# LayerNorm of the last 1024 tokens from x handed over in feature rows, in a fused attention and MLP kernel

## The chip, the cores and the metric

One core of a Trainium2 chip runs the whole kernel in one launch. The metric is the device time of one execution in microseconds (us): the median of 3 runs of the kernel before is 1620.89 us (1620.71 to 1621.32). The core's engines are TensorE (PE; its weight loads are PEld), VectorE (DVE), ScalarE (ACT), GpSimd (POOL) and SyncE (SP), which issues the DMAs here.

## The reference

```python
# x: [1, 2048, 512], 32 heads of 16; all float32
xn = (x - mean(x, -1)) / sqrt(var(x, -1) + 1e-5)
qkv = (xn @ wqkv).reshape(B, S, 3, H, Dh)            # wqkv: [512, 1536]
p = softmax(q @ k.T * Dh ** -0.5)                     # per head
s = (p @ v) @ wo                                      # wo: [512, 512]
h = xn @ w1 + b1; h = where(h > 0, h, 0) ** 2         # w1: [512, 1792]
g = silu(h @ w2 + b2)                                 # w2: [1792, 512]
return x + s * g
```

The inputs are drawn at random, x and the weights with a spread of 0.05, and b2 is multiplied by 3.878.

## The kernel before

Every float32 product is made of three matmuls in a reduced type: each operand is split in a high part (a copy, rounded) and a low part (what is left), and high x high, high x low and low x high are added up in PSUM. A product over 512 features takes 4 feature blocks x 3 = 12 matmuls.

The kernel has three stages. In the first one LayerNorm and some of the QKV projection are done. The 2048 tokens are 16 tiles of 128 (t = 0 to 15) and 4 chunks of 512 (c = 0 to 3). For each tile `load_x` brings x with tokens in rows, `ln_stats` takes mean and variance on VectorE (BN_STATS, BN_AGGR) and a square root on ScalarE, `ln_norm` normalizes, `ln_high` turns the tile with four TensorE transposes into PSUM (`pm_t`) and copies the high part to `xTs[c]` with ScalarE, and `ln_low` makes the low part with VectorE. `xTs[c]` has features in rows, as the projection needs them.

Between these the function `pump(n)` emits n matmuls of the projections that already have their tokens: `qk_tile(4, c)` makes K and `qk_tile(0, c)` Q of the first eight heads for chunk c (m = 4 and 0, 12 matmuls of 512 columns; chunk 0 is done in halves of 256 columns), `v_tile` makes V of one tile. They write to three PSUM banks of the pool `pe` in turn (`se`), and a bank is free when its result has been copied out. K and Q are split (`hl`), stored to DRAM (`k_d`, `q_d`), and read back in rows of heads: `load_k` fills the K tiles `ka` (12 DMAs, one row group of 16 partitions each), `load_q` the Q tiles `qm`. V goes to `v_d`. The normalized x is also copied to DRAM for the MLP (`spill`, to `xn_d`).

The second stage, the lead, interleaves the rest of the projections (L1157) with the first attention scores (L320), whose row maxima VectorE takes (L327). The third and longest stage is attention, and the MLP and output products between it.

PE, ACT, DVE and POOL run in the order in which the code is written. In the first stage the order of the DMAs on SP's queue is chosen when the program is built; SP then issues them strictly in that order, and a DMA that has to wait for a semaphore holds up all behind it. In the program each DMA also waits until the one that used its semaphore before (eight semaphores in turn) has landed.

The loop of the first stage is this, cut:

```python
for i in range(NT + 3):
    ...
    if i < NT:
        ln_stats(i)
    if 0 <= i - 1 < NT:
        ln_norm(i - 1)
    if 2 <= i - 3 < NT:
        ln_low(i - 3)
    if 0 <= i - 2 < NT:
        ln_high(i - 2)
```

Of the kernel before, what the change touches and what calls it, by code (L numbers as in the profile page):

```python
# [9 lines left out]
F32 = mybir.dt.float32  # L10
F32R = mybir.dt.float32r
AF = mybir.ActivationFunctionType
# [5 lines left out]
P = 128  # L18
S = 2048
# [13 lines left out]
NPT = 17  # L33
NVT = 7
NXR = 16
EVAC = (1, 6, 7, 9, 11, 14)
GAPS = (24,)
FIRST = 2
W1_LOADS = (13, 14, 16, 20, 23)
SPILLS = (5, 9, 13, 17)  # L40
LAST_MAX = 486
RUN = 454
PAIR = (484, 485)
# [14 lines left out]
def kernel(  # L58
# [6 lines left out]
    b1: bass.AP,  # L65
    w2: bass.AP,
    b2: bass.AP,
    out: bass.AP,
):
    nc = tc.nc  # L70
# [8 lines left out]
    r_d = [dram.tile([4, 512], F32, name=f"r_d{u}") for u in range(NU)]  # L79
    on_d = [dram.tile([2, P, S], F32, name=f"on_d{k}") for k in range(KO)]  # L80
    sp_d = dram.tile([S, D], F32, name="sp_d")
    xn_d = dram.tile([2, P, KO, S], F32, name="xn_d")
    v_d = dram.tile([P, NT, H * VW], F32, name="v_d")
    g_d = dram.tile([S, D], F32, name="g_d")
# [30 lines left out]
    with ExitStack() as ph:  # L115
# [39 lines left out]
                    src_d[h // 8][i, (h % 8) * DH : (h % 8 + 1) * DH, cols],  # L155
                )

        def load_k(qd, n):

            p, j, i = n // 6, n // 3 % 2, n % 3  # L160
            if n % 6 == 0:
                kas[qd, p] = ring("ka")
            h = 4 * qd + 2 * p + j
            nc.sync.dma_start(
                kas[qd, p][64 * j + DH * i : 64 * j + DH * (i + 1), :].bitcast(F32),
                k_d[h // 8][i % 2, (h % 8) * DH : (h % 8 + 1) * DH, :],
            )

        def load_v(qd):
# [830 lines left out]
        def load_w(name, width, parts):  # L1000
            raw = st.tile([P, KO, width], F32, name=name)
            at = 0
            for c0, n in parts:
                nc.sync.dma_start(raw[:, :, at : at + n], w_in[:, :, c0 : c0 + n])
                at += n
            return raw
# [11 lines left out]
        def qk_terms(m, c, ps):  # L1018
            wq, m0 = wq_cols(m)
            ms = slice(m0, m0 + P)  # L1020
            xT = xTs[c]
            t = terms3(ps, [
                (lambda a, q, ko=ko: wq[q, a, ko, ms], lambda b, q, ko=ko: xT[q, b, ko])
                for ko in range(KO)
            ])
            if m == 4 and c == 0:

                t = [t[k] for k in (0, 3, 6, 9, 2, 5, 1, 4, 7, 10, 8, 11)]
            return t

# [180 lines left out]
        xts = {}  # L1211

        def load_x(t):
            xts[t] = xp.tile([P, D], F32, name="xt", bufs=12)
            nc.sync.dma_start(xts[t], xf[t * P : (t + 1) * P, :])

        mvs = {}
        rstds = {}
        pts_ = {}

        def ln_stats(t):
            stats = xp.tile([P, 6], F32, name="stats")
            nc.vector.bn_stats(stats, xts[t])
            mvs[t] = xp.tile([P, 2], F32, name="mv", bufs=3)
            nc.vector.bn_aggr(mvs[t], stats)
            rstds[t] = xp.tile([P, 2], F32, name="rstd", bufs=3)
            nc.scalar.activation(rstds[t][:, 0:1], mvs[t][:, 1:2], AF.Sqrt, bias=eps_t)

        def ln_norm(t):
# [12 lines left out]
            xts[t] = xn  # L1242

        def ln_high(t):
            xn, xT = xts.pop(t), xTs[t // 4]
            pt = pm.tile([P, 512], F32, name="pm_t").rearrange("p (k n) -> p k n", n=P)
            for ko in range(KO):
                nc.tensor.transpose(pt[:, ko, :], xn[:, ko * P : (ko + 1) * P], ident)  # L1248
            sl = slice((t % 4) * P, (t % 4 + 1) * P)
            nc.scalar.activation(xT[:, 0, :, sl], pt, AF.Copy)  # L1250
            pts_[t] = pt
# [63 lines left out]
        make_ring("ka", kp, range(2), S)  # L1315
        for t in range(2):
            load_x(t)
        raw_m = load_w("wm", 2 * P, ((0, P), (D, P)))
        for t in range(2, 6):
            load_x(t)  # L1320
        raw_v = load_w("wv", D, ((2 * D, D),))
        for t in range(6, NT):
            load_x(t)
        for vt in vts:
            nc.vector.memset(vt[:, :, DH:], 1.0)
        fill_ring("ka", 0, -1.0)
        for i in range(NT + 3):
            if i in (2, 3):

                kos = slice(2 * i - 4, 2 * i - 2)  # L1330
                if i == 2:
                    ln_norm(1)
                    ln_high(0)
                    split_w(wa_t, kos, slice(0, 2 * P), raw_m[:, kos])
                    ln_low(0)
                else:
                    ln_high(1)
                    split_w(wa_t, kos, slice(0, 2 * P), raw_m[:, kos])
                    ln_stats(2)
                    ln_low(1)  # L1340
                    ln_norm(2)
                    ln_stats(3)
            else:
                if i < NT:
                    ln_stats(i)
                if 0 <= i - 1 < NT:
                    ln_norm(i - 1)
                if 2 <= i - 3 < NT:
                    ln_low(i - 3)
                if i == 4:  # L1350

                    pump(10)
                if 0 <= i - 2 < NT:
# [6 lines left out]
            if i in (11, 12):  # L1360
                fill_ring("qm", i - 11, 0.0)
            if i == 11:
                raw_r = [load_w("wv", 3 * P, ((P, 3 * P),))]
            if i in (13, 14):
                spill(0, i - 13)
            if i in (16, 18):
                spill(1, (i - 16) // 2)
            if i >= 4:
                pump({4: 6, 7: 14, 8: 12}.get(i, 8 if i < 7 else 7 if i < 11 else 6))
            if i == 3:  # L1370
                ahead.append(qk_first())
            if i >= 7 and (i - 3) % 4 == 3:
                c = (i - 3) // 4
                ahead.append(qk_tile(4, c))
                rest.append(qk_tile(0, c))
                order.append(("qk", 0, c))
            if i >= 3 and (i - 3) % 4 == 3:
                c = (i - 3) // 4
                rest += [v_tile(c, tt) for tt in range(4)]
                order += [("v", c, tt) for tt in range(4)]  # L1380
        let_go()
        hold[0] = False
        while ahead:
# [2 lines left out]
        kp2 = ph.enter_context(tc.tile_pool(name="kp2", bufs=1))  # L1386
        make_ring("ka", kp2, (2, 3), S)
        make_ring("qe", kp2, range(4), 512)
        for k in range(2):
# [5 lines left out]
            b1_t, b1.rearrange("(fo p) -> p fo", p=P), allow_slow_non_contiguous=True  # L1395
        )
        nc.sync.dma_start(b2_t, b2[None, :].to_broadcast([P, D]))
        for ko in range(KO):
            split_w(wr_t, ko, slice(0, 3 * P), raw_r[0][:, ko])
        for n in range(12):  # L1400
            load_k(0, n)
        qms[0] = load_q(0, "qm")
        fill_ring("qm", 2, 0.0)
        for n in range(4):
            fill_ring("qe", n, 0.0)
        fill_ring("ka", 2, -1.0)
        pump(47)
        led.append(0)
        at = order.index(("v", 2, 0)) + 1
        while len(rest) > len(order) - at:  # L1410
# [24 lines left out]
        def lead_rounds():  # L1435
            for i in side_rounds(specs, single):
                if i % 6 == 0:
                    now[0] = i // 6
                    run_waiting()
                    if i // 6 in SPILLS:  # L1440
                        c, k = divmod(SPILLS.index(i // 6), 2)
                        spill(c + 2, k)
# [263 lines left out]
        wstk.close()  # L1706


_INS = ['A_x', 'A_wqkv', 'A_wo', 'B_w1', 'B_b1', 'B_w2', 'B_b2']
_OUTS = [((1, 2048, 512), 'float32')]  # L1710


# [20 lines left out]
```

## Time and profile before

| | before |
|---|---|
| median of 3 runs | 1620.89 us (1620.71 to 1621.32) |
| profiled execution | 1621.38 us, span 1619.6 us, granted clock 1.00 |
| PE busy | 1607.3 us (99%) |
| PEld | 939.7 us (58%) |
| DVE | 1352.4 us (84%) |
| ACT | 1187.2 us (73%) |
| POOL | 534.1 us (33%) |
| chain that ended last | PE 99%, DVE 1% |
| first lead matmul (L1157) | 62.94 us after the span's start |

The profile is one execution; its times are counted from the start of the span, and 1.8 us of its 1621.38 us lie outside the span. A busy PE is not PE at its peak, since matmuls are pipelined. The chain that ended last is followed back from the last instruction, at each step to what released it. The queue of SP counts as no engine; the row of a DMA issue has the time that SP spent on it, waits for room in the queue included.

### The profile page before, as it was taken

Reading aid. Unit: us, or ns where it says so; the run is one execution under the profiler, and the core shown is the slowest. Engines: PE = TensorE matmul, PEld = TensorE weight load, DVE = VectorE, ACT = ScalarE, POOL = GpSimd, SP = SyncE. Lnnn points to the kernel's source line nnn. Section 1 sums busy time; section 2 is a strip of 40 time slices with the busy share of each in tenths; the row PEclk is TensorE's granted clock in tenths of the full one; section 3 lists DMA queues with packets and bytes.
Section 4 is the critical chain, followed back from the end, with each engine's and each line's share of the span. In section 5 each row is a group of like instructions: output and inputs, shape, how many; then the busy total and the mean of one; then the engine's idle time right before and its main releaser. Section 6 shows DMA issues by size and latency. Waiting matters only on the chain.

```text
span 1619.6 us, 36065 instructions
## 1 busy us (share of the span) xinstructions
PE 1607.3 (99%) x13660; PEld 939.7 (58%) x13660; DVE 1352.4 (84%) x2307; ACT 1187.2 (73%) x2347; POOL 534.1 (33%) x610
## 2 busy tenths in 40 slices
PE   8999999999999999999999999999999999999998
PEld 7799665556545654664466446645654565445543
DVE  7486888888888888888888888888888888887754
ACT  7212777777777777877777777777777777778886
POOL 6436667133113311331133113311331123214621
PEclk9999999999999999999999999999999999999999
DMA  8967556434333333423333334323432252237655
GB/s 290 244 237 234 174 156 160 132 96 128 81 104 94 106 88 88 131 87 101 90 107 100 91 89 118 115 71 90 131 107 73 65 163 76 64 102 228 207 177 169
DMA packets 164173, 209.19 MB, mean 129 GB/s; under 512 B 59136, under 2 KB 79360, under 8 KB 162432
## 3 DMA queue, kind: packets, MB, share of 16 engines
q1 hardware_dynamic: 163856, 206.63, 43.9%
q8 instruction: 108, 1.77, 0.5%
q14 instruction: 65, 0.53, 0.1%
q10 hardware_dynamic: 144, 0.26, 0.0%
HBM read 148.90 MB, written 56.34 MB: 127 GB/s over the span
## 4 chain that ended last, share of the span: by engine, by line
PE 99%; DVE 1%; DMA 0%; issue 0%; ACT 0%; DVEq 0%
PE po L406 31%; PE pd_t L258 19%; PE pm_t L320 17%; PE se L1286 15%; PE pd_t L226 5%; PE pm_t L1157 4%; PE pm_t L226 1%; PE pd_t L1157 1%; PE se L1127 1%; PE se L1061 1%; PE se L320 1%; PE pm_t L1248 0%; PE pd_t L1127 0%; DVE mx L327 0%; PE po L1061 0%; DMA xt<-in_A_x_dram 0%
## 5 line engine op out<-in xcount | busy, mean ns | idle before, releaser
L327 DVE TENSOR_REDUCE mx<-pm_t 128x1 f32<-128x512 f32 x1910 | 1188.3, 684 | 174.5 <-PE pm_t L320 84.8
L1298 ACT ACTIVATE pt<-se 128x512 f32<-128x512 f32 x1894 | 975.4, 613 | 234.3 <-PE se L1286 187.0
L320 PE MATMUL pm_t<-ka,qm 64*128 64x512 f32 x1910 | 761.0, 419 | 0.0
L1286 PE MATMUL se<-qe,ka 64*128 64x512 f32 x2005 | 677.3, 396 | 0.0
L406 PE MATMUL po<-pt,v 128*32 128x512 f32 x3820 | 520.8, 605 | 0.2 <-DVE tsm L849 0.2
L320 PEld LDWEIGHTS pm_t<-ka,qm 64*128 64x128 f32 x1910 | 335.2, 184 | 236.0 <-DVE mx L327 224.5
L1286 PEld LDWEIGHTS se<-qe,ka 64*128 64x128 f32 x2005 | 338.9, 184 | 19.8 <-ACT xr L1298 1.7
L258 PEld LDWEIGHTS pd_t<-xc,w1s 64*128 64x128 f32 x2352 | 292.1, 187 | 82.2 <-issue 82.2
L258 PE MATMUL pd_t<-xc,w1s 64*128 64x256 f32 x2352 | 332.3, 288 | 0.0
L258 PE MATMUL pd_t<-w2t,hT 64*128 64x512 f32 x1080 | 300.1, 410 | 0.0
L258 PEld LDWEIGHTS pd_t<-w2t,hT 64*128 64x128 f32 x1080 | 179.3, 184 | 82.4 <-issue 75.5
L571 POOL TENSOR_TENSOR r<-r 128x512 f32<-128x512 f32 x56 | 58.2, 1040 | 353.5 <-ACT r L568 353.5
L406 PEld LDWEIGHTS po<-pt,v 128*32 128x32 f32 x3820 | 76.7, 108 | 147.1 <-issue 125.6
L327 DVE TENSOR_REDUCE mx<-se 128x1 f32<-128x512 f32 x121 | 77.9, 686 | 26.1 <-PE pm_t L1157 17.3
L590 POOL TENSOR_TENSOR u<-u,b_t 128x512 f32<-128x512 f32 x16 | 20.6, 1285 | 209.1 <-ACT u L589 209.1
L568 ACT ACTIVATE r<-pd_t,b_t 128x256 f32<-128x256 f32 x112 | 46.9, 470 | 57.1 <-PE pd_t L258 55.0
L99 POOL TENSOR_SCALAR sh<-tr 128x32 fp32r<-128x32 f32 x30 | 6.5, 217 | 213.6 <-DVE tr L371 213.6
L1157 PE MATMUL pm_t<-xT,wr_t 64*128 64x512 f32 x408 | 74.0, 388 | 0.0
L100 POOL TENSOR_TENSOR hT<-r,hT 128x512 fp32r<-128x512 f32 x56 | 72.2, 1290 | 4.7
L226 PE MATMUL pd_t<-w2t,hT 64*128 64x512 f32 x264 | 68.7, 392 | 0.0
L1157 PEld LDWEIGHTS pm_t<-xT,wr_t 64*128 64x128 f32 x408 | 60.7, 185 | 0.0
L455 POOL TENSOR_TENSOR ot<-ot,hl 128x512 f32<-128x512 f32 x27 | 34.7, 1285 | 65.4 <-DMA hl<-r_d 51.7
(177 smaller groups left out, 1398.9 us busy)
## 6 DMA issues: line engine op xcount, KB each, us to landing
w1s<-w_d SPq DMA_DIRECT2D x196, 256.0 KB
qm<-q_d SPq DMA_DIRECT2D x384, 32.0 KB
ka<-k_d SPq DMA_DIRECT2D x96, 128.0 KB
qe<-q_d SPq DMA_DIRECT2D x384, 32.0 KB
q_d<-hl SPq DMA_DIRECT2D x16, 512.0 KB
g<-g_d SPq DMA_DIRECT2D x32, 256.0 KB
k_d<-hl SPq DMA_DIRECT2D x15, 512.0 KB
on_d<-hl SPq DMA_DIRECT2D x116, 64.0 KB
```

Of the source, the lines that this page charges most:

```text
L100: (lo or nc.gpsimd).tensor_tensor(dst[1], raw, dst[0].bitcast(F32), op=ALU.subtract)
L226: mm = nc.tensor.matmul(out_, lh(r), rh(r), start=first_ and lane == 0, stop=last_ and lane == 1, skip_group_check=True,)
L258: mm = nc.tensor.matmul(out_, lh(r), rh(r), start=first_ and lane == 0, stop=last_ and lane == 1, skip_group_check=True,)
L320: nc.tensor.matmul(ps, qms[u][p][64 * j : 64 * j + 64, qb * P : (qb + 1) * P], kas[qd, p][64 * j : 64 * j + 64, kc * 512 : (kc + 1) * 512] ...
L327: return nc.vector.tensor_reduce(mxs[u][:, c, kc : kc + 1], ps, axis=AX.X, op=ALU.max)
L406: nc.tensor.matmul(po[32 * j : 32 * j + 32, :], vs[qd][:, (4 * kb + j) * VW : (4 * kb + j) * VW + 32], pts[j], start=(kb == 0), stop=(kb = ...
L455: nc.gpsimd.tensor_tensor(ot, ot, rb, op=ALU.mult)
L568: nc.scalar.activation(r[:, i], ps[:, i * CW : (i + 1) * CW], AF.Relu, bias=b1_t[:, fo : fo + 1])
L571: nc.gpsimd.tensor_tensor(r, r, r, op=ALU.mult)
L1157: mm = nc.tensor.matmul(out_, lh(r), rh(r), start=first_ and lane == first, stop=last_ and lane != first, skip_group_check=True,)
L1286: nc.tensor.matmul(se, kas[qd, j // 2][b : b + 64, kb * P : (kb + 1) * P], qes[u][j // 2][b : b + 64, :], start=True, stop=True,)
L1298: return nc.scalar.activation(pts[j], se, AF.Exp, scale=0.25)
```

## The change

The host hands over two more arrays: `A_x_t`, x of the last 1024 tokens with features in rows, in pieces of 256 tokens, and `A_wqkv_m`, the first 128 columns of Q and K of the weights side by side. Chunks 0 and 1 are normalized as before. For chunks 2 and 3 the statistics are still taken from tiles with tokens in rows (`ln_stats`), but means and reciprocal deviations of a chunk are collected in `lns`, turned into rows (`ln_rows`), written to DRAM (`ln_d`), and read back to all 128 partitions (`ln_back`, tile `lnr`, 128 x 1024). `ln_half(c, h)` subtracts and multiplies 256 tokens of x in feature rows (`xr_`, two buffers, brought by `load_xt`) on VectorE, copies the high part with ScalarE and makes the low part with GpSimd. The transposes, `ln_norm`, `ln_high` and `ln_low` of tiles 8 to 15 are gone. K's first tiles are loaded in two halves of 1024 tokens, the first before K of chunks 2 and 3 is made. The x tiles have 8 buffers instead of 12, the copies to `xn_d` come later, and the order of the matmuls within K's tiles of chunks 1 to 3 puts those with the low part of x last.

```diff
+        def ln_rows(c):
+            m = lns[c]
+            nc.scalar.activation(m[:, 4:8], m[:, 4:8], AF.Sqrt, bias=eps_t)
+            nc.vector.reciprocal(m[:, 4:8], m[:, 4:8])
+            tr = xp.tile([P, 32], F32, name="lnt")
+            nc.vector.transpose(tr, m)
+            for q in range(4):
+                nc.sync.dma_start(
+                    ln_d[c].rearrange("k t n -> (k t) n")[:, 32 * q : 32 * q + 32],
+                    tr[32 * q : 32 * q + 8],
+                )
+        def ln_back(c):
+            row = lnrs[c] = xp.tile([P, 2, 512], F32, name="lnr")
+            nc.sync.dma_start(
+                row.rearrange("p k n -> p (k n)"),
+                ln_d[c].rearrange("k t n -> (k t n)")[None, :].to_broadcast([P, 1024]),
+            )
+        def ln_half(c, h):
+            ns = slice(256 * h, 256 * h + 256)
+            row, raw, xT = lnrs[c], xrs.pop((c, h)), xTs[c]
+            pairs = (slice(0, 2), slice(2, 4))
+            for kos in pairs:
+                for k, op in ((0, ALU.subtract), (1, ALU.mult)):
+                    nc.vector.tensor_tensor(
+                        raw[:, kos], raw[:, kos], row[:, k : k + 1, ns].to_broadcast([P, 2, 256]), op=op
+                    )
+                nc.scalar.activation(xT[:, 0, kos, ns], raw[:, kos], AF.Copy)
+            for kos in pairs:
+                nc.gpsimd.tensor_tensor(
+                    xT[:, 1, kos, ns], raw[:, kos], xT[:, 0, kos, ns].bitcast(F32), op=ALU.subtract
+                )
...
-        for i in range(NT + 3):
+        for i in range(11):
...
+        add_chunk(1)
         let_go()
         hold[0] = False
+        ln_stats(15)
+        ln_rows(3)
+        ln_half(2, 0)
+        load_xt(3, 0)
+        pump(12)
+        ln_back(3)
+        ln_half(2, 1)
+        load_xt(3, 1)
+        for n in range(2):
+            fill_ring("qm", n, 0.0)
+        pump(12)
+        ln_half(3, 0)
+        pump(12)
+        for n in range(12):
+            load_k(0, n, slice(0, 1024))
+        ln_half(3, 1)
+        qms[0] = load_q(0, "qm")
+        pump(12)
+        add_chunk(2)
+        raw_r = [load_w("wv", 3 * P, ((P, 3 * P),))]
+        pump(12)
+        add_chunk(3)
+        pump(12)
...
+        for n in range(12):
+            load_k(0, n, slice(1024, S))
```

The order on TensorE around the middle of the first stage, before. `xT0` to `xT2` are the chunks' normalized x; matmuls into `pm_t` are transposes, `se_550` is K of chunk 1, `se_656` K of chunk 2:

```order
L1061 MATMUL se_550<-xT1_193,wa_t_190 128x512 x6
L1248 MATMUL pm_t_568<-ident_141,xn_533 128x128 x4
L1061 MATMUL se_550<-xT1_193,wa_t_190 128x512 x6
L1248 MATMUL pm_t_593<-ident_141,xn_563 128x128 x4
L1127 MATMUL se_606<-wa_t_190,xT0_192 128x512 x6
L1248 MATMUL pm_t_624<-ident_141,xn_588 128x128 x4
L1127 MATMUL se_606<-wa_t_190,xT0_192 128x512 x6
L1248 MATMUL pm_t_648<-ident_141,xn_619 128x128 x4
L1061 MATMUL se_656<-xT2_194,wa_t_190 128x512 x6
```

And now; `se_559`, `se_681` and `se_698` are K of chunks 1, 2 and 3, `se_662` is Q of chunk 1, and the rows on `wa_t,xT0` are V of chunk 0:

```order
L1133 MATMUL se_513<-wa_t_192,xT0_194 128x512 x12
L1067 MATMUL se_559<-xT1_195,wa_t_192 128x512 x12
L1133 MATMUL se_592<-wa_t_192,xT0_194 128x512 x12
L1133 MATMUL se_615<-wa_t_192,xT0_194 128x512 x12
L1067 MATMUL se_662<-xT1_195,wa_t_192 128x512 x12
L1067 MATMUL se_681<-xT2_196,wa_t_192 128x512 x12
L1067 MATMUL se_698<-xT3_193,wa_t_192 128x512 x12
L1133 MATMUL se_715<-wa_t_192,xT1_195 128x512 x12
```

The transposes of tiles 8 to 15 are gone, and the matmuls of K of chunks 2 and 3 stand at the end of what was emitted so far, one behind the other.

The order on SP's queue where the means and deviations of chunk 2 pass through DRAM, now; `wv_679` are weights for the lead, `xt` tiles 13 to 15 of x, `b1` and `b2` biases, `k_d0` and `q_d0` stores of K and Q of chunk 0:

```order
L1008 DMA wv_679<-in_A_wqkv_dram 128x4x384
L1221 DMA xt_384<-in_A_x_dram 128x512
L1221 DMA xt_413<-in_A_x_dram 128x512
L1221 DMA xt_445<-in_A_x_dram 128x512
L1490 DMA b1_t_150<-in_B_b1_dram 128x14x1
L1493 DMA b2_t_151<-in_B_b2_dram 128x512
L1363 DMA xn_d_136<-xT0_194 512x1x256
L1020 DMA k_d0_61<-hl_462 128x2x512
L1251 DMA ln_d2_134<-lnt_486 8x32 x4
L1020 DMA q_d0_57<-hl_502 128x2x512
L1145 DMA v_d_137<-vt0_201 128x544
L1258 DMA lnr_509<-ln_d2_134 128x1024
```

Before, the same stretch of the queue held the weights, two copies to `xn_d`, the biases and the store of K, and nothing that TensorE's next matmuls waited for:

```order
L1004 DMA wv_548<-in_A_wqkv_dram 128x4x384
L1310 DMA xn_d_134<-xT0_192 512x1x256 x2
L1394 DMA b1_t_148<-in_B_b1_dram 128x14x1
L1397 DMA b2_t_149<-in_B_b2_dram 128x512
L1016 DMA k_d0_61<-hl_449 128x2x512
```

What moved is that the small stores `ln_d2` and the load `lnr_509` stand behind all of these.

On VectorE the four operations of each `ln_half` stand so; `hl_572` is the split of K of chunk 1, which frees the bank that Q of chunk 1 (`se_662`) takes:

```order
L1249 STREAM_TRANSPOSE lnt_543<-lns3_198 128x32
L1269 TENSOR_TENSOR xr__236<-xr__236,lnr_509 128x512 x4
L110 TENSOR_TENSOR hl_572<-se_559,hl_572 128x512
L1269 TENSOR_TENSOR xr__238<-xr__238,lnr_509 128x512 x4
L1269 TENSOR_TENSOR xr__557<-xr__557,lnr_576 128x512 x4
L1269 TENSOR_TENSOR xr__586<-xr__586,lnr_576 128x512 x4
L110 TENSOR_TENSOR hl_675<-se_662,hl_675 128x512
```

`xr__236` and `xr__238` are the two halves of chunk 2, `xr__557` and `xr__586` those of chunk 3; before, VectorE had a subtraction of 128x512 and three small operations for each tile in their place.

More of the change, by code (lines that the diff above doesn't have):

```diff
@@ L81 @@
     sp_d = dram.tile([S, D], F32, name="sp_d")
+    ln_d = {c: dram.tile([2, 4, P], F32, name=f"ln_d{c}") for c in (2, 3)}
     xn_d = dram.tile([2, P, KO, S], F32, name="xn_d")
@@ L1218 @@
         rstds = {}
+        lnrs = {}
+        xrs = {}
+        lns = {c: xp.tile([P, 32], F32, name=f"lns{c}", bufs=1) for c in (2, 3)}
+        for m in lns.values():
+            nc.vector.memset(m, 1.0)
         pts_ = {}
@@ L1227, in ln_stats, with load_xt @@
             nc.scalar.activation(rstds[t][:, 0:1], mvs[t][:, 1:2], AF.Sqrt, bias=eps_t)
+        def ln_rows(c):
[29 more added lines that the diff above has]
+                )
+        def load_xt(c, h):
+            raw = xrs[c, h] = xp.tile([P, KO, 256], F32, name="xr_")
+            nc.sync.dma_start(raw, x_t[c - 2, h])
         def ln_norm(t):
@@ L1317 @@
             load_x(t)
-        raw_m = load_w("wm", 2 * P, ((0, P), (D, P)))
+        raw_m = st.tile([P, KO, 2 * P], F32, name="wm")
+        for k in (0, 2):
+            nc.sync.dma_start(raw_m[:, k : k + 2], w_m[:, k : k + 2])
         for t in range(2, 6):
@@ L1321 @@
         raw_v = load_w("wv", D, ((2 * D, D),))
-        for t in range(6, NT):
+        for t in range(6, 8):
             load_x(t)
+        for h in range(2):
+            load_xt(2, h)
         for vt in vts:
@@ L1326, with add_chunk @@
         fill_ring("ka", 0, -1.0)
-        for i in range(NT + 3):
+        def add_chunk(c):
+            if c:
+                ahead.append(qk_tile(4, c))
+                rest.append(qk_tile(0, c))
+                order.append(("qk", 0, c))
+            rest.extend(v_tile(c, tt) for tt in range(4))
+            order.extend(("v", c, tt) for tt in range(4))
+        for i in range(11):
             if i in (2, 3):
-                kos = slice(2 * i - 4, 2 * i - 2)
                 if i == 2:
                     ln_norm(1)
+                    load_x(9)
                     ln_high(0)
-                    split_w(wa_t, kos, slice(0, 2 * P), raw_m[:, kos])
+                    split_w(wa_t, slice(0, 2), slice(0, 2 * P), raw_m[:, 0:2])
                     ln_low(0)
@@ L1337 @@
                     ln_high(1)
[L1338 removed]
+                    split_w(wa_t, slice(2, 4), slice(0, 2 * P), raw_m[:, 2:4])
                     ln_stats(2)
@@ L1359 @@
                 fill_ring("ka", 1, -1.0, (32 + 64 * (i - 9),))
[L1360 to L1367, printed above, removed]
+            if i == 9:
+                ln_back(2)
             if i >= 4:
-                pump({4: 6, 7: 14, 8: 12}.get(i, 8 if i < 7 else 7 if i < 11 else 6))
+                pump({4: 6, 7: 14, 8: 12}.get(i, 8 if i < 7 else 7))
             if i == 3:
                 ahead.append(qk_first())
[L1372 to L1380, printed above, removed]
+            if i == 6:
+                add_chunk(0)
+        add_chunk(1)
+        let_go()
+        hold[0] = False
+        ln_stats(15)
[21 more added lines that the diff above has]
+        pump(12)
         let_go()
@@ L1397 @@
         nc.sync.dma_start(b2_t, b2[None, :].to_broadcast([P, D]))
[L1398 to L1403, printed above, removed]
+        for k in range(2):
+            spill(0, k)
         for n in range(4):
```

59 lines of the change are left out of this document (45 added, 14 removed).

## The prediction

> **What bounds the kernel now.** I read the page's chain first, then the chain of waits of the first 70 us in order of time, then busy time by stage. The page's chain says who decides the end:
>
> ```profile
> PE 99%; DVE 1%; DMA 0%; issue 0%; ACT 0%; DVEq 0%
> ```
>
> TensorE is the chain from end to end, so what delays it anywhere goes through to the end one for one. The change touches the first stage and the way into the lead, so that is where its worth must be read. The chain there (start, length, what; x is the count):
>
> ```profile
> 0.74 2.75 DMA xt<-in_A_x_dram
> ...
> 9.02 2.60 PE se L1061 x10
> 11.61 0.85 PE pm_t L1248 x4
> ...
> 14.60 1.12 PE se L1061 x8
> ...
> 16.16 0.95 PE se L1061 x8
> 17.11 0.44 PE pm_t L1248 x4
> ...
> 22.21 0.44 PE pm_t L1248 x4
> 22.65 1.63 PE se L1127 x7
> ...
> 24.28 0.44 PE pm_t L1248 x4
> ...
> 37.32 0.44 PE pm_t L1248 x4
> 37.75 2.79 PE se L1127 x12
> ...
> 60.13 2.80 PE pd_t L1127 x12
> 62.94 0.43 PE pm_t L1157
> ...
> 63.90 5.55 DVE mx L327 x9
> ```
>
> From 9 us on TensorE never waits until the lead starts at 62.94 us. Twelve matmuls of 512 columns cost 2.80 us (0.233 us each), four transposes 0.44 us. The groups from 24.28 to 37.32 are the transposes of tiles 8 to 15, eight groups. In the lead VectorE's maxima pace TensorE for 5.55 us; the change leaves that order as it is. Busy time by stage:
>
> ```profile
> core 0: us, PE busy (x) PEld busy (x) DVE busy (x) ACT busy (x) POOL busy (x), PEclk, DMA share, GB/s
> ...
> 10.00:20.00 10.00, 10.00 (x68) 9.96 (x68) 9.33 (x30) 8.57 (x17) 8.16 (x9) 1.00 0.82 303
> 20.00:40.40 20.40, 20.40 (x109) 16.86 (x108) 13.90 (x40) 15.86 (x32) 13.25 (x15) 1.00 0.86 291
> ```
>
> The DMA queue is nearly full as well (share 0.82 and 0.86 at about 300 GB/s), which matters since the change puts a new path through it.
>
> **What goes.** Eight groups of transposes at 0.44 us: 3.5 us of TensorE. If nothing else happened the lead would start at 59.4 us. This is all that the change can win: VectorE's and ScalarE's work on these tiles lay beside TensorE.
>
> **What is added: a path of waits.** TensorE now does what is left of V of chunk 0, K of chunk 1, two more V tiles, and then needs Q of chunk 1, K of chunk 2 and K of chunk 3, in this order. The last transposes (tile 7) still end at 22.65 us; behind them stand 2 + 12 + 12 + 12 + 12 = 50 matmuls, 11.7 us, so TensorE reaches Q of chunk 1 at 34.3 us. K of chunk 3 would end at 42.7 us if all were there. I follow the path that feeds it.
>
> First the means and deviations of chunk 2. VectorE has them early:
>
> ```profile
> 20.52 0.68 DVE L1256 TENSOR_TENSOR xT<-pm_t,xT 128x512 fp32r<-128x512 f32 x1
> 21.12 0.68 DVE L1223 BATCH_NORM_STATS2 stats<-xt 128x6 f32<-128x512 f32 x1
> ```
>
> The first is the low part of tile 6, when the statistics of ten tiles were done; the changed order has twelve by about then, and some 22.5 us is when the rows are ready to be stored. But the store stands on SP's queue behind the weights of the lead, three x tiles, two biases, half a copy to `xn_d` and a store of K. The weights wait for GpSimd to leave their buffer. GpSimd's row and SP's rows of before:
>
> ```profile
> 8.61 2.52 POOL L996 TENSOR_TENSOR wa_t<-wm,wa_t 128x512 fp32r<-128x512 f32 x2 [3.59 <-ACT wa_t L995]
> 12.64 0.62 POOL L99 TENSOR_SCALAR wa_t<-wv 128x512 fp32r<-128x512 f32 x1 [1.51 <-DMA wv<-in_A_wqkv_dram]
> ...
> 19.20 1.29 POOL L100 TENSOR_TENSOR wa_t<-wv,wa_t 128x512 fp32r<-128x512 f32 x1
> ```
>
> ```profile
> 20.52 0.38 SPq L1004 DMA_DIRECT2D wv<-in_A_wqkv_dram  x1
> 20.99 3.40 SPq L1310 DMA_DIRECT2D xn_d<-xT  x2
> 24.44 0.69 SPq L1394 DMA_DIRECT2D b_t<-in_B_b_dram  x1
> 25.18 3.59 SPq L1397 DMA_DIRECT2D b_t<-in_B_b_dram  x1
> 28.87 0.38 SPq L1016 DMA_DIRECT2D k_d<-hl  x1
> ...
> 47.48 0.38 SPq L1016 DMA_DIRECT2D k_d<-hl  x1
> ...
> 51.61 6.42 SPq L164 DMA_DIRECT2D ka<-k_d  x12
> ```
>
> The fullest stretch of the queue, for a bound:
>
> ```profile
> 30.00:40.00 10.00, 10.00 (x55) 8.32 (x54) 5.81 (x15) 7.15 (x14) 4.54 (x8) 1.00 1.03 382
> ```
>
> GpSimd's four splits last 7.9 us (12.64 to 20.49). The weights of Q and K now come in long rows and free the queue sooner, so the splits could begin at the end of the row at 8.61, 11.1 us, and end at 19.0. Behind the weights lie 0.79 MB of weights, 0.79 MB of x, 0.26 MB of bias, 0.52 MB of copy and 0.52 MB of K: 2.9 MB, at 300 GB/s 9.6 us. With 2.75 us for a DMA alone (the row at 0.74), and the few small stores behind, these land at 19.0 + 9.6 + 2.75 + about 2 = 33.5 us. SP's issue of the bias took 3.59 us before, so I don't expect less. The load `lnr` may be issued only then; it is 0.5 MB to 128 partitions, behind a store of Q and one of V in the queue: 2.75 us and 1.3 us for the bytes, landing at 37.5 us. Bounds: 32.5 us, if SP is held up by nothing but what the program orders (x tile 15 lands at 19.0 + 2.75 + 1.58 MB at 382 GB/s = 25.9; a store and the load of what it stored took 51.61 - 47.48 = 4.1 us to the load's issue at most and 2.75 at least; then the load); 40 us, if the weights still leave at 20.52 and the broadcast load takes a microsecond more.
>
> From there on durations, from the groups by form:
>
> ```profile
> L815 DVE TENSOR_TENSOR g<-g,s 128x512 f32<-128x512 f32 x12 | 8.8, 741 | 0.3
> L106 DVE TENSOR_TENSOR hl<-se,hl 128x512 fp32r<-128x512 f32 x2 | 1.4, 692 | 7.0 <-ACT hl L105 7.0
> L105 ACT ACTIVATE hl<-se 128x512 fp32r<-128x512 f32 x2 | 1.2, 597 | 2.8 <-PE se L1061 2.2 <-issue 0.6
> L1250 ACT ACTIVATE xT<-pm_t 128x512 fp32r<-128x512 f32 x16 | 9.5, 593 | 4.9 <-PE pm_t L1248 4.4
> L100 POOL TENSOR_TENSOR hl<-raw,hl 128x512 fp32r<-128x512 f32 x5 | 6.5, 1292 | 0.4
> ```
>
> VectorE's operation on two tiles of 128x512 took 0.74 us, of which a little overlaps: an `ln_half` of four is 2.8 us (2.4 at 0.60 from start to start, as between the two VectorE rows above). Counted from the landing of `lnr` (37.5):
> - `ln_half(2, 0)` 2.8, ScalarE's second copy 0.6, its copy of K of chunk 1 0.6, VectorE's split of the same 0.7. Sum 4.7: only now, at 42.2 us, is the bank free that Q of chunk 1 needs. TensorE has stood since 34.3.
> - `ln_half(2, 1)` 2.8, ScalarE 0.6, GpSimd's last low part 1.3. Sum 9.4.
> - x of the second half of chunk 3 goes to the buffer that GpSimd has just left (two buffers `xr_`); 0.5 MB, 2.75 + 0.65 = 3.4. Sum 12.8.
> - `ln_half(3, 1)` 2.8, ScalarE 0.6. Sum 16.2: K of chunk 3 may begin. Its first eight matmuls take 1.9 us, and GpSimd's low part comes 1.3 us after ScalarE, so it runs through: 2.8. Sum 19.0, at 56.5 us.
>
> Behind it stand six tiles of 12 matmuls (V of chunk 1, Q and a V tile of chunk 2), 16.8 us, as before from 46.14 to 62.94. The lead starts at 73.3 us instead of 62.94: 10.4 us late, the 3.5 us already counted in.
>
> **What costs nothing.** K's second halves: K of chunk 3 is at 56.5, split 1.3, stored and asked for 4.1 later, 61.9; the first tile's six loads may take as long as all twelve took to the first maximum before, 51.61 to 63.90, and a half of that is 6, so 68 against a lead at 73.3; the copies of x to `ka` stand between them and take 2.8 at 382 GB/s. If that cover of 2.5 us goes, the lead waits for the difference. The weights of Q and K in longer rows help nothing: the first matmul waits for ScalarE, not for them. The moved copies to `xn_d` and fills of `qe` lie beside TensorE's lead. Each of these I take as 0, with +-1 us.
>
> **The sum.** 1621.38 us of the profiled execution + 10.4 = 1631.8; that execution lies 0.5 us above the median, so 1631.3 us for the runs; I round to 1631.5.
>
> **The rivals.** What can be told from no change is about 0.2%, 3.2 us.
> - *The table is early.* `lnr` at 32.5: the same path, 5 us less, +5.4 us: 1626.3. For it: three of the five things ahead are stores and small. Against: 3.40 and 3.59 us of SP's own issue rows. With 2.4 instead of 2.8 us for three `ln_half` another 1.2 less: 1625.
> - *TensorE comes back slow.* In the chain above four transposes took 0.85 us at 11.61 and 0.44 at 17.11, at a granted clock of 1.00 in both stretches: eight matmuls of 256 columns took 1.12 at 14.60 and 0.95 at 16.16. At its start TensorE runs at half speed, until some 14.8 us; of the 5.8 us from 9.02 on that loses 2.9. Two waits arise here, 8 us before Q of chunk 1 and about 4 before K of chunk 3 (K of chunk 2 ends near 50, K of chunk 3 begins at 53.7). After the first one the slow part falls into time in which it would wait anyway. If the second one makes it slow too, 2.9 more: +13.3, 1634.2, and with `lnr` at 40 1636.7. No row of before shows a wait of this length after the start. The Trainium skill, TensorE: Matmul & The Clock Gate, Part 1, has the clock halved after at least one idle window of about 3.4 us, free-running; by that the first wait surely does it and the second only when a window falls wholly into its 4 us.
> - *Faster: the pieces come in time.* TensorE loses the 3.5 us of transposes and waits for nothing: 1617.4. The place is the landing of `lnr`: 19.0 + 16.8 us stand behind it, so the lead is no later than before if it lands by 27.1 us, and gets all by 23.6. For it: the statistics are there at 22.5, and the DMA queue lies idle around 20. Against: SP's order, in which tile 15 of x alone lands later than that.
> - *Even*: `lnr` at about 27, or a part of the path shorter than I have it: 1621.
>
> **How the numbers follow.** Main case 0.55; early table 0.20; slow return 0.15; in time 0.05; even 0.05. The main case is the likeliest: 1631.5. The range takes the two slower neighbours in and leaves the last two out: low 1625, high 1637. Faster by over 0.2% 0.05, within 0.05, slower 0.90.
>
> **What would show it.** In the changed profile: the chain of the first 75 us has a wait of TensorE before Q of chunk 1 from about 34 to 42 us, and one before K of chunk 3 ending near 54; the first row of L1163 stands near 73 us; VectorE's first L1269 is released by the DMA `lnr` near 37.5; the stretch after the lead's start is as long as before. A first L1163 at 59 to 63 us would show the whole path wrong, one near 68 the early table. Four matmuls at twice the spacing after the second wait would show the slow return.

## The result, and the profile after

The changed kernel took 1635.2 us (median of 4 runs, 1634.9 to 1636.5) against 1621.0 us (4 runs): ratio 1.0089, 95% interval 1.0072 to 1.0106. The forecast was 1631.5 us, range 1625 to 1637. The profiled execution took 1634.87 us, span 1633.1 us (before 1621.38 and 1619.6). Two far slower runs of the kernel before, of 1913.7 and 3022.8 us, taken beside the experiments, are left out of every ratio and spread below.

The chain of waits of the changed kernel, in order of time (start, length, what):

```profile
30.65 1.77 DMA ln_d<-lnt
...
32.50 4.20 DMA lnr<-ln_d
...
36.73 0.70 DVE xr__236 L1269
...
40.66 0.69 DVE hl L110
41.35 1.04 DVE xr__238 L1269
...
43.84 3.01 POOL xT L1274 x2
...
46.87 4.25 DMA xr__586<-in_A_x_t_dram
...
51.22 1.15 DVE xr__586 L1269
...
54.45 0.64 ACT xT L1272
55.09 0.04 issue
55.13 3.89 PE se L1067 x10
59.02 2.78 PE se L1133 x12
...
75.76 0.43 PE pm_t L1163
```

This is the forecast path, station by station: the table of chunk 2 through DRAM, two halves on VectorE, GpSimd's low part, the load of x into the buffer just left, the last half, K of chunk 3, six more tiles. TensorE's waits on it (in total, times, longest):

```profile
PE se L1067 <- DVE hl L110: 7.4, 1, 7.4
PE se L1067 <- ACT xT L1272: 5.1, 1, 5.1
```

These two waits are 12.5 us, and the lead starts at 75.76 instead of 62.94, 12.8 us late. That the two numbers are so close is chance. TensorE was 3.7 us ahead when the first wait began (at 33.96; 108 matmuls of 0.233 us were left to the lead, 59.1 against 62.9), since the transposes are gone; and those 108 matmuls took some 4.0 us longer than that, because some ran at half clock and K of chunk 3 paused once more between the two copies of its last half: Q of chunk 1 and K of chunk 2 took 7.3 us instead of 5.6, K of chunk 3 took 5.2 instead of 2.8. So it is 12.5 + 4.0 - 3.7 = 12.8. At the end the distance is 13.5 us; where the other 0.7 us arise, behind the lead's start, stays open.

The same stretch in pieces of 3.41 us (columns: PE, PEld, DVE, ACT, POOL busy, then granted clock, DMA share, GB/s):

```profile
34.13:37.54 3.41, 0.00 (x0) 0.00 (x0) 0.78 (x2) 0.00 (x0) 0.00 (x0) 1.00 0.84 261
37.54:40.95 3.41, 0.00 (x0) 0.00 (x0) 2.19 (x4) 1.75 (x3) 2.00 (x2) 0.50 0.46 159
40.95:44.37 3.42, 2.96 (x7) 2.39 (x8) 3.35 (x5) 0.63 (x1) 1.41 (x2) 0.50 0.33 92
44.37:47.78 3.41, 3.41 (x15) 2.60 (x15) 1.27 (x3) 1.12 (x2) 3.30 (x4) 1.00 0.81 298
47.78:51.19 3.41, 0.93 (x4) 0.40 (x3) 1.63 (x3) 1.75 (x3) 3.22 (x5) 1.00 0.51 176
51.19:54.61 3.42, 0.81 (x2) 0.50 (x2) 3.13 (x4) 0.79 (x2) 1.40 (x2) 0.50 0.66 197
54.61:58.02 3.41, 3.30 (x8) 2.31 (x8) 1.29 (x2) 1.44 (x3) 2.21 (x2) 0.50 0.38 113
58.02:61.43 3.41, 3.41 (x17) 2.75 (x16) 0.69 (x1) 2.25 (x5) 1.23 (x2) 1.00 0.25 74
```

Each clock value fills whole pieces: a piece with little or no work is followed by one at 0.50, and 0.50 lasts until a piece has been busy. After the second wait K of chunk 3 runs at half clock: eight matmuls in a piece, where the last row has seventeen.

### The profile page after: what moved, and what is told of

Read it like the earlier page. It is cut to its first block, busy times and chain, and to the rows that moved or that the text cites. A ratio compares the mean times of both kernels' runs of the same rounds, so it can differ in the third digit from the quotient of the medians.

```text
span 1633.1 us, 36021 instructions
## 1 busy us (share of the span) xinstructions
PE 1607.8 (98%) x13628; PEld 937.6 (57%) x13628; DVE 1358.9 (83%) x2307; ACT 1180.9 (72%) x2333; POOL 542.9 (33%) x614
## 4 chain that ended last, share of the span: by engine, by line
PE 96%; DVE 2%; DMA 1%; ACT 0%; POOL 0%; issue 0%; SPq 0%; DVEq 0%
PE po L410 31%; PE pd_t L262 20%; PE pm_t L324 16%; PE se L1339 14%; PE pd_t L230 5%; PE pm_t L1163 4%; PE pm_t L230 1%; PE pd_t L1163 1%; PE se L324 1%; DMA xt<-in_A_x_dram 1%; PE pd_t L1133 1%; DVE stats L1234 0%; DVE mx L331 0%; DMA xr__586<-in_A_x_t_dram 0%; DMA lnr<-ln_d 0%; PE se L1067 0%
```

## Experiments

Each is the changed kernel with the edit shown, unless it says otherwise. Theory: TensorE waits for the path of the table, and every step of the path counts in full. Rivals: TensorE's bank, the bytes in the DMA engines, the clock, GpSimd's company.

**K of chunk 1 copied out ahead of the table.** The bank for Q of chunk 1 is then free early.

```diff
         ln_rows(3)
+        pump(12)
         ln_half(2, 0)
         load_xt(3, 0)
-        pump(12)
         ln_back(3)
```

> The matmuls of K of chunk 1, and with them its split on ScalarE and VectorE, are emitted ahead of ln_half(2, 0), so the bank for Q of chunk 1 comes free near 30.5 us and TensorE's wait before Q of chunk 1 (7.45 us) goes. Theory of the path (statistics, four ln_half, x buffers): the path only loses the 1.8 us between ln_half(2, 0) and ln_half(2, 1); the wait moves to K of chunk 2; the lead starts near 73.9 instead of 75.7 us and the run takes 1633.4 us (1632.5 to 1634.3). Rival, the bank is what costs: all 7.5 us of the first wait come back, 1628 us.

Measured: 1636.3 us, ratio 1.0093 (1.0079 to 1.0108). This is neither the theory nor the rival. TensorE's waits:

```profile
PE se L1067 <- ACT vt L1142: 9.4, 1, 9.4
PE se L1067 <- ACT xT L1272: 3.3, 2, 2.7
```

Q of chunk 1 no longer waits, but ScalarE's copy of a V tile stands behind both halves of chunk 2 (it starts at 45.79), so K of chunk 2 waits for that bank instead. The step between the two halves is gone, and yet the path from the table to the last copy takes 18.1 us against 18.4 in the changed kernel, since without the step the second half runs beside GpSimd's low part of the first:

```profile
37.80 2.75 DVE L1269 TENSOR_TENSOR xr__236<-xr__236,lnr 128x512 f32<-128x512 f32 x4 [6.50 <-DMA lnr<-ln_d]
40.47 4.75 DVE L1269 TENSOR_TENSOR xr__238<-xr__238,lnr 128x512 f32<-128x512 f32 x4
```

The second half took 4.75 us, the first one, alone, 2.75. The table landed at 37.8 in this profile, 1.1 us later than in the changed kernel, which is why the lead starts later here (76.77).

**The table on ScalarE's queue.**

```diff
-                nc.sync.dma_start(
+                nc.scalar.dma_start(
                     ln_d[c].rearrange("k t n -> (k t) n")[:, 32 * q : 32 * q + 32],
...
-            nc.sync.dma_start(
+            nc.scalar.dma_start(
                 row.rearrange("p k n -> p (k n)"),
```

> The stores of means and deviations and the load of the table to all partitions are issued from ScalarE's queue, not from SP's. Theory of the path: the stores leave right after the transpose (22.9 us, not 28.1 to 31.0), the table lands near 30.5 instead of 36.7 us, everything behind moves by as much, the lead starts 5 to 7 us earlier, 1629 us (1627.5 to 1631). Rival, the table is late because the DMA engines are full or the broadcast is slow by itself: it lands after 34 us and the run stays above 1632.5 us.

Measured: 1638.1 us, ratio 1.0102 (1.0087 to 1.0116). This is the rival, and worse: the table landed at 38.7, 2.0 us later. ScalarE's rows (start, then the length; for the issue of a DMA, ACTq, the length has its waits in it):

```profile
22.83 5.84 ACTq L1251 DMA_DIRECT2D ln_d<-lnt  x4
28.71 0.60 ACT L1303 ACTIVATE xT<-pm_t 128x512 fp32r<-128x512 f32 x1 [6.38 <-DMA xt<-in_A_x_dram]
```

The stores were asked for from 22.83 on, 5.2 us earlier than in the changed kernel, and the last of them landed at 32.41, the same time as there (32.42). Stores and x share the DMA engines. The Trainium skill, DMA: Bandwidth & Descriptors, "Issuing engines are not separate DMA queues", says that DMAs of different engines end on the same 16 DMA engines; this trace agrees, but its remark that the time to issue is usually small beside the DMA itself does not hold here: the four stores kept ScalarE from other work for 5.84 us, and TensorE waited 3.6 us for a ScalarE copy. So my reading of SP's order as the cause was only a part of it: the backlog ahead of the stores is the other.

**x of chunk 3's first half in another buffer** (that of the weights of Q and K, which are done with). SP's queue then has the last x tiles ahead of the weights of the lead, and the biases and the copy to `xn_d` behind the table.

```diff
         def load_xt(c, h):
-            raw = xrs[c, h] = xp.tile([P, KO, 256], F32, name="xr_")
+            if (c, h) == (3, 0):
+                raw = xrs[c, h] = raw_m
+            else:
+                raw = xrs[c, h] = xp.tile([P, KO, 256], F32, name="xr_")
```

> x of chunk 3's first half goes to the buffer of the weights wm (done with at 11 us), so it needn't wait for GpSimd, and the second half takes the buffer that ln_half(2, 0) leaves. As built, the two biases and the copy to xn_d also come behind the table on SP's queue. Theory of the path: from the table to the end of ScalarE's last copy 14.7 us instead of 18.4 (the waits of VectorE for x, 2.1 and 1.8 us, go), and the table lands about 3 us earlier: 1628.5 us (1627 to 1631). Rival, x buffers don't matter and only the queue does: the 3 us of the table alone, 1632 us, with VectorE still idle before L1269 on chunk 3.

Measured: 1631.6 us, ratio 1.0063 (1.0049 to 1.0077). This is between the two, nearer the rival. VectorE:

```profile
32.26 2.75 DVE L1269 TENSOR_TENSOR xr__236<-xr__236,lnr 128x512 f32<-128x512 f32 x4 [4.47 <-DMA lnr<-ln_d]
36.79 3.18 DVE L1269 TENSOR_TENSOR xr__238<-xr__238,lnr 128x512 f32<-128x512 f32 x4
39.89 4.80 DVE L1269 TENSOR_TENSOR wm<-wm,lnr 128x512 f32<-128x512 f32 x4
44.61 5.78 DVE L1269 TENSOR_TENSOR xr__585<-xr__585,lnr 128x512 f32<-128x512 f32 x4
```

The table lands 4.5 us earlier with less ahead of it, and x never makes VectorE wait; but the last two halves take 4.80 and 5.78 us beside GpSimd, and 3.2 us are left of the gain in the lead's start (72.53).

**TensorE kept busy with 20 matmuls that nobody reads, ahead of K of chunk 3.**

```diff
+        idle = pm.tile([P, 512], F32, name="pm_t")
+        for _ in range(20):
+            nc.tensor.matmul(
+                idle, wa_t[:, 0, 0, :P], xTs[0][:, 0, 0], start=True, stop=True
+            )
         add_chunk(3)
         pump(12)
```

> 20 matmuls of 512 columns that nobody reads stand between K of chunk 2 and K of chunk 3, 4.7 us in the wait of 5.1 us. Theory of the clock: the granted clock stays at 1.00 there, the last ten matmuls of K of chunk 3 take about 2.4 instead of 3.7 us, 1633.8 us (1633.2 to 1634.4). Rival, the low part from GpSimd sets the pace of these matmuls: they still end near 58.9 us, 1635.2 us.

Measured: 1635.0 us, ratio 1.0084 (1.007 to 1.0099). The time says the rival, the trace doesn't:

```profile
55.90 0.64 ACT xT L1272
56.54 0.04 issue
56.59 2.59 PE se L1067 x10
59.18 2.78 PE se L1133 x12
```

The clock was 1.00 here, and from the last copy to the end of K of chunk 3 it took 2.6 us instead of 3.9: the half clock costs 1.3 us in this place. In this execution the table landed at 38.1, 1.4 us later than in the profile of the changed kernel, and the two cancel. The landing was at 36.7 to 38.1 in the profiles of the kernels that have it in the same place; that all the runs of this kernel had it late isn't shown, so how much the unread matmuls bring in the median stays open.

**Low parts by VectorE.**

```diff
-                nc.gpsimd.tensor_tensor(
+                nc.vector.tensor_tensor(
                     xT[:, 1, kos, ns], raw[:, kos], xT[:, 0, kos, ns].bitcast(F32), op=ALU.subtract
```

> Changed kernel with the low parts of the new halves taken by VectorE instead of GpSimd; the work on VectorE grows by four 128x512 operations a chunk. Theory (the path is slower than forecast because VectorE and GpSimd slow each other, and because GpSimd's pair of 3.0 us holds x's buffer): halves 2.8 us each without company, low parts 1.4 us more, x's buffer free at 45.9 instead of 46.9 and the low part of the last half some 2 us earlier: lead 1 to 2 us earlier, 1633 to 1634.5 us. Rival (company costs nothing, VectorE's longer work is all that counts): two times 1.4 us more on the path, 1636.5 us or more.

Measured: 1633.8 us, ratio 1.0076 (1.0064 to 1.0089). This is the theory.

```profile
46.54 2.75 DVE L1269 TENSOR_TENSOR xr__557<-xr__557,lnr 128x512 f32<-128x512 f32 x4
49.20 1.48 DVE L1274 TENSOR_TENSOR xT<-xr__557,xT 128x512 fp32r<-128x512 f32 x2
50.64 2.75 DVE L1269 TENSOR_TENSOR xr__586<-xr__586,lnr 128x512 f32<-128x512 f32 x4
```

Alone, every half takes 2.75 us, and with its low part 4.2, less than the 4.8 that a half took beside GpSimd. K of chunk 3 begins at 52.8 instead of 53.8, though the table landed 1.1 us later than in the changed kernel. That the two engines exclude each other is what the Trainium skill states, SBUF — State Buffer, "SBUF: two separate sides": a VectorE operation with two inputs in SBUF and a GpSimd operation that reads SBUF share a port pair as an exclusive lock for a whole instruction. The rows agree: an operation of 0.70 us took 1.04 to 1.76 us, that is up to one more GpSimd operation of 1.3 us, and beside GpSimd's fills, which read nothing, a half took 2.91.

**K's rows loaded whole** (loads of the first halves gone, `load_k(0, n)` in the place of the second).

```diff
-        for n in range(12):
-            load_k(0, n, slice(0, 1024))
...
-            load_k(0, n, slice(1024, S))
+            load_k(0, n)
```

> Changed kernel with K's rows for the first tiles loaded whole, in the place of the second halves; the loads of the first halves are gone. Theory (the halves cost nothing and bring nothing here, since the lead starts at 75.7 and the first tile's second halves had landed by 74): 1634.5 to 1636 us. Rival (whole rows come later than the lead): the first tile's six loads carry twice the bytes and land after 76, 1637 us or more. Rival (the loads at 51 to 57 us take VectorE's or the queue's time from x): 1634 us or less.

Measured: 1635.2 us, ratio 1.0089 (1.0075 to 1.0103), in the median the same as with halves. Two of the five runs took 1637.4 and 1638.1 us. The profile is of the slowest: the table landed 1.0 us later than in the changed kernel, the lead started at 77.70, and TensorE did not wait for K's rows. So this part of the change neither cost nor brought anything that these runs show.

**Another order of the same work.** V tiles, which need no new piece, are emitted ahead of the first half and between the halves, Q of chunk 1 behind K of chunk 3; the fills and loads of `qm` move behind K of chunk 2. The edit, cut:

```diff
         ln_rows(3)
+        ln_back(3)
+        pump(36)
         ln_half(2, 0)
         load_xt(3, 0)
         pump(12)
-        ln_back(3)
         ln_half(2, 1)
...
-        ln_half(3, 1)
-        qms[0] = load_q(0, "qm")
         pump(12)
+        ln_half(3, 1)
         add_chunk(2)
+        pump(12)
+        for n in range(2):
+            fill_ring("qm", n, 0.0)
+        qms[0] = load_q(0, "qm")
```

> Changed kernel with another order of the same work: three more tiles (V of chunk 0, V of chunk 1) are emitted ahead of the first ln_half, the other V tiles of chunk 1 between the halves, Q of chunk 1 behind K of chunk 3. Theory (TensorE loses only what it waits for pieces; work that needs no new piece can stand in the wait): the table lands at 36.7 as before, K of chunk 3 begins near 54 and ends near 58, but only Q of chunk 1, Q of chunk 2 and one V tile stand behind it (8.4 us), so the lead starts at 66 to 69 instead of 75.7, its first maxima waiting for K's second halves: 1626 to 1629 us. Rival (the copies out of the banks stand behind the halves on ScalarE and VectorE, so V of chunk 1 stops TensorE just so): a gain below 2 us, 1633.5 or more.

Measured: 1634.1 us, ratio 1.0079 (1.0066 to 1.0092). This is the rival's time, but not by its mechanism: the lead started at 68.1, 7.6 us earlier, as the theory has it, and gave it back. The chain:

```profile
60.94 2.98 POOL wr_t L1000 x3
63.92 0.28 SPq L157
64.30 0.37 SPq L1145
64.77 3.13 DMA k_d<-hl
...
70.99 3.53 DMA ka<-k_d
74.52 0.24 issue
74.76 0.76 PE se L324
```

The store of K of chunk 3 stood on SP's queue behind twelve loads of Q, which began only at 57.3, with GpSimd's fills, and took SP 6.9 us, and K's second halves, hidden in the changed kernel, now held TensorE for 4.3 us just behind the lead's start; after that wait the clock is 0.50 again.

**The same order, and x early in the other buffer** (the edits of both).

> As the kernel with the other order, and x of the first half of chunk 3 loaded early into the buffer that the weights of Q and K have left, so that it waits for no buffer and the biases and the copy of x stand behind the table on SP's queue. Theory: the table lands at 32.2 as in the kernel with that buffer alone, VectorE does three halves without a wait for x, TensorE reaches K of chunk 3 at 48 and finds it by 51; end 54, lead near 62.5 with up to 2.5 us of waiting for K's second halves: 1621 to 1624 us, that is within 3 us of the kernel before. Rival (VectorE beside GpSimd is so slow that three halves in a row gain nothing): K of chunk 3 not before 55, 1626 us or more.

Measured: 1627.5 us, ratio 1.0041 (1.0028 to 1.0053). It is slower than the theory's range and in the rival's, but K of chunk 3 began at 48.5, not after 55, so the rival's mechanism is not it: it is again K's halves; without them the lead would have been 1.4 us ahead of the kernel before (first maximum at 62.53 against 63.90). TensorE's waits and SP's rows:

```profile
PE se L324 <- DMA ka<-k_d: 5.1, 1, 5.1
PE se L1067 <- ACT xT L1272: 0.8, 2, 0.6
```

```profile
51.47 6.69 SPq L157 DMA_DIRECT2D qm<-q_d  x12
58.25 0.37 SPq L1145 DMA_DIRECT2D v_d<-vt  x1
58.71 0.38 SPq L1020 DMA_DIRECT2D k_d<-hl  x1
```

**The last with Q's tiles filled and loaded early; the same with VectorE's low parts; and that with the copies behind K's halves.**

```diff
         load_xt(3, 0)
+        for n in range(2):
+            fill_ring("qm", n, 0.0)
         pump(36)
         ln_half(2, 0)
+        qms[0] = load_q(0, "qm")
```

> As the kernel with the other order and the early x of chunk 3, but the tiles for Q of the first heads are filled by GpSimd before the first half and loaded before K's first halves. In the kernel without this, TensorE was ready for the lead 1.4 us earlier than in the kernel before and then waited 5.1 us for K's second halves, because the store of K of chunk 3 stood on SP's queue behind twelve loads of Q that waited for GpSimd. Theory (what is left of the loss is that place in the queue): the store goes at 54 instead of 58.7, the wait falls to 0 to 1.5 us: 1622 to 1624 us. Rival (the bytes of the copies to ka ahead of the second halves hold them, not the queue's order): a gain below 2 us, 1625.5 us or more.

> As the kernel before in this list, and the low parts of the new halves by VectorE. A half beside GpSimd took 4.8 us on VectorE in a row of three; alone 2.75, with the low parts 4.2. Theory (the two engines cost each other more than VectorE's four more operations): K of chunk 3 may begin 1 us earlier, lead's wait shorter by as much: 1621 to 1623 us. Rival (K of chunk 3 is by then held by TensorE's own order, not by VectorE): no difference from the kernel without it, within 0.5 us; slower by over 1 us if the low part of chunk 2 comes late for K of chunk 2.

> As the kernel with the low parts by VectorE, and the two copies of x to ka, the biases and the copies to xn_d stand on SP's queue behind K's second halves instead of ahead of them. Theory (copies and halves share the DMA engines): the second halves land 1 to 2 us earlier and the lead waits for nothing; it starts at 60.5 to 61.5 against 62.94 in the kernel before: 1619 to 1621.5 us. Rival (the stores of Q of chunks 1 and 2, which now stand ahead of the halves, hold them until 59.5, and the copies come late for the lead): 1622 us or more.

Measured: 1623.8 us (11 runs, ratio 1.0015, 1.0006 to 1.0024), 1623.4 us (11 runs, 1.0013, 1.0004 to 1.0022) and 1626.7 us (7 runs, 1.0032, 1.0021 to 1.0044). The first is the theory: the place on SP's queue was worth 3.7 us. The second is the rival, within 0.4 us of the first: x of the last half lands only at 47.9 and 47.5, so VectorE's speed no longer decides. The third is its rival: stores of Q now hold the halves, which TensorE awaits for 2.3 us.

The first two differ by 2.6 us in their profiled spans (1622.3 and 1619.7) with nearly the same waits of TensorE, 2.7 and 2.5 us. A part of that is the clock. The first, around its wait, then the second (in whose profile the clock never changes on the way, so that its pieces are cut at the wait):

```profile
47.92:51.33 3.41, 0.72 (x2) 0.30 (x2) 2.63 (x4) 1.31 (x3) 1.30 (x1) 1.00 0.39 111
51.33:54.74 3.41, 3.41 (x8) 2.76 (x9) 0.69 (x1) 0.93 (x2) 1.68 (x2) 0.50 0.66 241
```

```profile
47.77:51.00 3.23, 0.74 (x3) 0.30 (x3) 3.07 (x6) 1.32 (x3) 0.00 (x0) 1.00 0.41 113
51.00:54.50 3.50, 3.50 (x15) 2.87 (x16) 1.47 (x3) 1.75 (x4) 0.00 (x0) 1.00 0.65 237
```

The 22 matmuls behind the wait took 6.92 us in the first and 5.39 in the second:

```profile
51.33 6.92 PE L1067 MATMUL se<-xT,wa_t 128*128 128x512 f32 x22 [0.60 <-ACT xT L1272]
```

```profile
51.00 5.39 PE L1067 MATMUL se<-xT,wa_t 128*128 128x512 f32 x22 [0.59 <-ACT xT L1272]
```

So the clock is 1.5 of the 2.6 us; 0.3 more come from the wait ending later, and 0.8 behind the lead's start are not explained. The runs of the two kernels spread over 1.8 and 3.0 us, those of the kernel before, which waits nowhere here, over less than 1. The mean granted clock of each run is on record (3.41 us at half clock lower it by 0.001), and it parts the runs of the second kernel: the three at 1.000 took 1621.5 to 1622.1 us, the eight at 0.998 or 0.999 took 1623.3 to 1624.5. In the first kernel all eleven are at 0.998 or 0.999 and still spread over 1.8 us; in the kernel before 0.999 and 1.000 both occur and do not part the runs. So the clock goes with the larger step, and not with all of the spread.

**And x of the last half asked for ahead of Q** (on the kernel with VectorE's low parts).

```diff
         ln_half(2, 0)
-        qms[0] = load_q(0, "qm")
+        load_xt(3, 1)
         pump(12)
         ln_half(2, 1)
-        load_xt(3, 1)
         pump(12)
         ln_half(3, 0)
+        qms[0] = load_q(0, "qm")
```

> As the kernel with the other order, the early x of chunk 3, the early fills and the low parts by VectorE, but the load of x of the last half stands on SP's queue ahead of the loads of Q, whose place it had behind: in that kernel it was asked for at 41.3 and landed at 47.5, though its buffer was free at 36.3, and TensorE waited 2.5 us for K of chunk 3. Theory (the last wait is that place in the queue, and the spread of those runs, 1621.5 to 1624.5, is whether a slow half-clock window of TensorE follows that wait): x lands near 40, K of chunk 3 is there at 46 when TensorE reaches it at 47.6, no wait, no slow window, the lead starts at 60.4 against 62.94 in the kernel before: span 1617.4, 1618.5 to 1620.5 us, all runs within 1 us of each other. Rival (K's second halves or the lead's own data become the bound in the wait's place): 1620.5 to 1622 us; the spread stays if the slow window has another cause.

Measured: 1623.1 us (11 runs), ratio 1.001 (1.0001 to 1.0019). It is above both ranges, by 1.0 us even above the rival's, and the spread of 2.9 us (1621.2 to 1624.1) stayed; what holds the lead is what the rival said. TensorE runs through K of chunk 3 without a wait and starts the lead at 59.3, and then

```profile
PE se L324 <- DMA ka<-k_d: 3.7, 1, 3.7
```

K's second halves again: Q's loads moved the loads of the first halves back, SP issued these until 53.3, and the store of K of chunk 3 went at 54.9, though VectorE's split was done at 52.4. The wait moved from K of chunk 3 to these halves, and in this profile half clock follows it there (0.50 from 66 to 69). No kernel here beats the one before; the nearest are 0.1% slower.

## Why the prediction was right, and where it was off

- **TensorE is the chain, and the first stage decides: right.** The lead's delay of 12.8 us is the whole difference but for 0.7.
- **The table at 37.5: right** (36.7 in this execution, up to 38.1 in others), but partly by luck, since two errors nearly cancel. The weights left SP at 20.2, not 19.0, since GpSimd's splits began at 12.3 and not at 11.1; and from there the stores had landed after 12.2 us, not after 14.5.
- **The path from the table to K of chunk 3, 16.2 us: mis-sized, 18.4.** The order of the steps was right. The second half and GpSimd's pair took 5.5 instead of 4.7, the load of x 4.25 instead of 3.4, the last half with its copy 3.9 instead of 3.4. I took VectorE's and GpSimd's operations from rows in which the other was not in the way.
- **The slow return: came true, at less than half its price.** I had it as a rival of 0.15 and 2.9 us; K of chunk 3 took 3.9 us after its release instead of 2.8, and the unread matmuls took 1.3 of that away. The path was 2.2 us longer than forecast, the table 0.8 earlier and K of chunk 3 1.1 slower, so the lead came 2.5 us late against the forecast. With the 0.7 us behind it that is 3.1 of the 3.7 us between 1631.5 and 1635.2; the other 0.6 is that the median lies 0.3 us above the profiled run, not 0.5 below it, less 0.2 of rounding. The measured time is nearer to this rival's 1634.2 than to the main case, yet the longer path made more of the difference than the clock.
- **Costs nothing: right.** K's halves (whole rows: the same time); the first tile's second halves landed by 74.0, 1.8 us ahead of the lead. The cover was not large: in four of the eight kernels whose lead came earlier TensorE waited for these halves next, for 2.3 to 5.1 us.
- **The gain of 3.5 us: not refuted.** The last kernel, in which TensorE waits for nothing from 10 us on up to the lead, starts it 3.6 us earlier than the kernel before (59.3 against 62.9).
- **"In time", "even" and the early table did not happen.** The table at 32 was reached only by another order on SP, and then VectorE beside GpSimd took back part of it.

## What to carry to other kernels

Work taken off the bounding engine is only won if what replaces it arrives in time: before moving a step to other engines, follow its path to the first instruction that needs it, through every queue, and count each round trip through DRAM (here 28.1 to 36.7 for 4 KB). When a wait is filled, look for the next late thing at once; here the same few microseconds reappeared as a bank, as x, as K's halves and as the clock. On a queue that issues in order, small and urgent transfers should stand ahead of bulk that nobody awaits (the table landed 4.5 us earlier so). Where two engines hinder each other, compare with one that does both parts (4.2 us against 4.8 here), and see whether anything waits for it: in the last order it changed the time by 0.4 us.

## What had not been expected of the hardware

- Half clock comes without a fully idle piece: 0.93 us of work in 3.41 (the changed kernel), or 0.72 (the kernel with Q's tiles early) and 1.04 (the one with the copies behind K's halves), were followed by one or two pieces at 0.50. In the changed kernel the four changes of the clock lie on one grid of 3.41 us. The Trainium skill, TensorE: Matmul & The Clock Gate, Part 1, has a free-running window of that length, which the grid bears out; that the window must be idle is too strict by these rows, and my condition that one falls wholly into the wait was wrong.
- VectorE and GpSimd on operands in SBUF: a half of 2.75 us took 4.75 to 4.84 beside GpSimd's low parts, and up to 5.78.
- Four stores of 1 KB each kept the issuing engine for 2.9 us on SP and 5.8 us on ScalarE while bulk was ahead of them.
